# The order of the first units in a fused RWKV attention and cosine router

## Chip, cores and metric

The kernel runs on one core of one Trainium2 chip, in one launch. The metric is device time in microseconds, from the first to the last instruction of a run. The kernel before takes 399.03 us (median of three runs, 398.66 to 399.29).

In the profile PE is TensorE's matmuls and PEld its weight loads, DVE is VectorE, ACT is ScalarE, POOL is GpSimd, and SP is SyncE, which issues the loads. A matmul of float32 appears as two records.

## The reference

An attention with a decaying state, and then a mixture of experts with one expert per token. Cut to what matters:

```python
# r, k, v: (4, 8, 768, 48); w, u: (8, 48)
for t in range(S):
    kt, vt, rt = k[:, :, t], v[:, :, t], r[:, :, t]
    cur = einsum('bhd,bhe->bhde', u * kt, vt)           # the token's own term
    y[:, :, t] = einsum('bhd,bhde->bhe', rt, state + cur)
    state = w * state + einsum('bhd,bhe->bhde', kt, vt)
x = y as rows: (3072, 384)
logits = normalised(x) @ normalised(expert_emb).T / tau   # 8 experts
expert = argmax(logits); gate = softmax(logits)[expert]
out[token] = gate * (relu(x[token] @ w1[expert]) @ w2[expert])
```

## The kernel before

The sequence of 768 is cut into 6 chunks of 128 tokens; with 4 batches that makes 24 units, numbered chunk by chunk. A "step" i works on several units at once: it turns the R and K of unit i+1, sums unit i, scales the K of a coming unit, and ranks the tokens of a group (the four units of one chunk) that was finished some steps earlier. The instructions of each engine run in the order in which the program issues them, and an engine that waits holds everything behind it.

The start loads, computes the powers of the decay, and prepares unit 0:

```python
    wide = k.work.tile([128, 512], F32, name="wide", tag="AT1")
    nc.vector.memset(wide, 1.0)
    def busy(columns):                       # idle products that keep TensorE busy
        ps = k.ps.tile([128, 512], F32, name="wake", tag="y")
        nc.tensor.matmul(ps[:, 0:columns], k.ones, wide[:, 0:columns], start=True, stop=True)
    for _ in range(WAKE):                    # WAKE = 2
        busy(512)
    ...
    load(k, 0, k.Kpad[0])                    # K of unit 0 goes straight to its padded tile
    ...
    own_k(k, 0)
    for p in range(NP):                      # NP = 4: powers of the decay by scans over C = 128
        nc.vector.tensor_tensor_scan(
            t[:, p, :], wc[:, p : p + 1].to_broadcast([128, C]), k.ones, 1.0, ALU.mult, ALU.mult
        )
    ...                                      # mid, kp, rpow, turned K and R of unit 0
    busy(192)
    nc.scalar.copy(k.kpow..., ps...)         # powers by which K is scaled
    nc.vector.tensor_mul(first, first, ps[:, :, :, 0:D])     # K of unit 0, scaled in place
```

The pieces of a step that the change moves or that stand beside them:

```python
def load(k, i, K=None):                      # on SyncE: K, R, (u with unit 0), V
    ...
    if i == 0:
        k.u_bc = ...
        nc.sync.dma_start(out=k.u_bc..., in_=u broadcast to 128 partitions)
    for n in () if i == 0 else (0, 1) if i == 1 else (i,):
        nc.sync.dma_start(out=k.loaded[n][2], in_=of(k.v, n % B))

def scaled(k, i):                            # needs K of unit i and kpow
    k.nc.gpsimd.tensor_mul(k.Kpad[i % 4][:, :, 0:D], k.loaded[i][0], k.kpow)

def own_k(k, i):                             # needs K of unit i and u
    k.nc.gpsimd.tensor_mul(k.KU[i], k.loaded[i][0], k.u_bc)

def own_r(k, i):
    k.nc.gpsimd.tensor_mul(k.KU[i], k.KU[i], k.loaded[i][1][:, :, 0:D])

def own_sum(k, i):
    k.nc.vector.reduce_sum(diag, k.KU.pop(i), axis=AX.X)

def ranks(k, g):                             # PSUM tag "tp": two banks, also of rt, yrows, lgT
    g.rank = k.ps.tile([128, E, B], F32, name="rank", tag="tp")
    mm(g.rank, k.umask, g.oh, start=True, stop=False)
    mm(g.rank, k.ones, g.pre, start=False, stop=True)
```

The step itself, cut (`whole(f, i - n)` runs f for a group whose last unit is i - n; `on(f, i)` runs f for unit i):

```python
    for i in range(-1, units):
        if 0 < i + AHEAD < units:            # AHEAD = 5
            load(k, i + AHEAD)
        whole(places, i - 4)
        ...
        on(turn_r, i + 1)                    # rt: L360, then RT: L362
        if i == 0: own_sum(k, i)
        on(turn_k, i + 1)                    # kt: L369
        ...
        on(scaled, i + 2)                    # L317
        if i < 0:
            own_r(k, 0)
        on(own, i + 2)                       # L328, L332
        ...
        whole(located, i - 4)
        ...
        on(own_sum, i + 1)                   # diag: L337
        on(sums, i)                          # y: L443 (from chunk 1 on), L452
        on(states, i)                        # st: L409
        on(carry, i)                         # state: L422 or L424, then L425 on POOL
        on(scores, i + 1)                    # at: L388
        on(masked, i + 1, 0)                 # AT: L394
        if i == 0: masked(k, i + 1, 1)
        on(rows, i)                          # yrows: L470, then X: L476
        if i != 0: on(masked, i + 1, 1)
        of_group(put, i)                     # X to memory
        of_group(turn_rows, i - 1)           # xp: L556
        whole(logits, i - 2)
        whole(ranks, i - 3)                  # rank: L625, L626
        if i == 0: build_constants(k)        # small memsets on POOL
```

## Time and profile before

| | |
|---|---|
| time | 399.03 us (398.66 to 399.29) |
| span of the profiled run | 396.4 us, 9266 instructions |
| TensorE's granted clock, mean | 0.997 |
| 24 to 36 us: busy PE, DVE, ACT, POOL | 11.73, 9.58, 10.57, 11.59 of 12.00 |
| 113 to 158 us: busy PE, DVE, ACT, POOL | 44.37, 27.46, 19.81, 17.46 of 45.00 |
| 158 to 396 us: busy PE, DVE, ACT, POOL | 232.17, 136.11, 70.88, 53.98 of 238.00 |
| starts of the scores (L388) of units 0 to 4 | 7.50, 11.28, 15.25, 19.55, 23.85 |

The attention takes the first 130 us or so, the experts the rest. A step's length is the distance from one start of the scores to the next. In the table the start is where several engines are full at once, and the experts are TensorE's alone. Shares over the whole span hide this difference: they are read by stretch.

### The profile page before, as it was taken

The page shows a single profiled execution, that of the slowest core. Times are in us where ns is not written, and L with a number is a line of the kernel's source. Part 1 is how long each engine was busy: PE and PEld are TensorE (multiplying, and loading weights), DVE is VectorE, ACT ScalarE, POOL GpSimd, SP SyncE. Part 2 cuts the span into 40 slices and gives each one's busy share as a digit, 9 for nine tenths or more (in the row PEclk, how much of TensorE's full clock was granted, in tenths as well). Part 3 has the DMA queues.
Part 4 walks back from the last instruction along what each step waited for, and adds up shares of the span by engine and source line. Part 5 has one row for each costly group of instructions (what it writes and reads, how often), then busy time and mean ns, then how long its engine had stood idle before and what let it go on. Part 6 is the DMA issues. An engine that isn't in the chain of part 4 may idle for free.

```text
span 396.4 us, 9266 instructions
## 1 busy us (share of the span) xinstructions
PE 386.9 (98%) x3542; PEld 352.5 (89%) x3542; DVE 253.2 (64%) x600; ACT 173.1 (44%) x524; POOL 160.9 (41%) x216
## 2 busy tenths in 40 slices
PE   7999999999999999999999999999999999999993
PEld 4988888889888877899999999999999999799783
DVE  6887878787788670757667668257275456655601
ACT  4887777777677412333333332233323243133120
POOL 7998796858664232500701502220350350200111
PEclk9999999999999999999999999999999999999998
DMA  7899887767606972244705532434164170150111
GB/s 146 163 215 214 189 180 162 157 136 149 142 33 206 288 285 65 87 161 163 255 7 215 196 106 94 133 112 161 55 227 159 43 237 3 40 180 0 41 39 44
DMA packets 93797, 54.35 MB, mean 137 GB/s; under 512 B 76938, under 2 KB 88381, under 8 KB 93747
## 3 DMA queue, kind: packets, MB, share of 16 engines
q1 hardware_dynamic: 90242, 44.26, 41.4%
q0 software_dynamic: 3296, 9.44, 7.3%
q8 instruction: 29, 0.48, 0.5%
q14 instruction: 22, 0.17, 0.1%
q10 hardware_dynamic: 208, 0.00, 0.0%
HBM read 44.45 MB, written 9.63 MB: 136 GB/s over the span
## 4 chain that ended last, share of the span: by engine, by line
PE 86%; SPq 4%; ACT 3%; DMA 2%; DVE 2%; POOL 1%; issue 1%; POOLq 0%; DVEq 0%; ACTq 0%
PE ps L1226 25%; PE ps L1290 18%; PE ps L1330 5%; PE at L388 4%; PE ps L1344 4%; PE y L452 4%; PE early_h L1036 3%; PE early_y L1045 3%; PE ps L1204 3%; PE yrows L470 2%; PE ps L1174 2%; PE y L443 2%; PE rt L360 2%; PE kt L369 2%; PE xp L556 2%; PE st L409 2%
## 5 line engine op out<-in xcount | busy, mean ns | idle before, releaser
L1090 POOL DMA_INDIRECT out_dram<-y,to x25 | 30.1, 1204 | 173.5 <-DVE Sh L1365 109.9
L1226 PE MATMUL ps<-xTe,w 128*128 128x192 f32 (+3 forms) x336 | 62.9, 327 | 0.0
L1226 PEld LDWEIGHTS ps<-xTe,w 128*128 128x128 f32 x336 | 55.9, 190 | 0.5
L346 ACT ACTIVATE xd<-V,diag 128x48 f32<-128x48 f32 x184 | 46.2, 326 | 0.1
L394 DVE TENSOR_TENSOR AT<-at,umask 128x512 f32<-128x512 f32 x48 | 32.7, 685 | 10.5 <-PE at L388 10.3
L1233 ACT ACTIVATE hT<-hT 128x384 f32<-128x384 f32 (+3 forms) x42 | 22.0, 523 | 32.4 <-DVE hT L1256 19.7
L1290 PE MATMUL ps<-Tw,Sh 128*128 128x192 f32 x192 | 32.5, 326 | 0.0
L1290 PEld LDWEIGHTS ps<-Tw,Sh 128*128 128x128 f32 x192 | 31.4, 190 | 0.0
L1081 POOL DMA_INDIRECT G<-xs,take x25 | 27.0, 1080 | 10.5 <-issue 4.6
L1226 PE MATMUL ps<-Tx,Sw 128*128 128x192 f32 (+3 forms) x168 | 29.7, 326 | 0.0
L388 PE MATMUL at<-RT,KT 48*128 48x128 f32 x384 | 27.9, 285 | 0.3 <-DVE RT L362 0.3
L1243 DVE TENSOR_TENSOR u<-ps,p 128x384 f32<-128x384 f32 (+3 forms) x14 | 7.8, 558 | 31.3 <-ACT p L1240 16.6
L1226 PEld LDWEIGHTS ps<-Tx,Sw 128*128 128x128 f32 x168 | 27.6, 190 | 0.1
L452 PE MATMUL y<-AT,V 128*48 128x128 f32 (+1 forms) x384 | 26.0, 278 | 0.0
L388 PEld LDWEIGHTS at<-RT,KT 48*128 48x128 f32 x384 | 23.3, 187 | 2.6 <-issue 0.7
L332 POOL TENSOR_TENSOR KU<-KU,Rpad 128x384 f32<-128x384 f32 x24 | 24.1, 1004 | 1.8
L452 PEld LDWEIGHTS y<-AT,V 128*48 128x48 f32 (+1 forms) x384 | 19.9, 124 | 4.2 <-issue 3.6
L1290 PE MATMUL ps<-w,hT 128*128 128x192 f32 x128 | 23.4, 326 | 0.0
L328 POOL TENSOR_TENSOR KU<-K,u_bc 128x384 f32<-128x384 f32 x23 | 23.2, 1008 | 0.0
L317 POOL TENSOR_TENSOR Kpad<-K,kpow 128x384 f32<-128x384 f32 x23 | 23.1, 1004 | 0.1
L558 ACT COPY xT<-xp 128x384 f32<-128x384 f32 x24 | 11.5, 479 | 25.5 <-PE xp L556 25.5
L1253 ACT ACTIVATE hT<-ps 128x384 f32<-128x384 f32 (+3 forms) x14 | 6.9, 490 | 35.7 <-PE ps L1226 35.7
(240 smaller groups left out, 816.5 us busy)
## 6 DMA issues: line engine op xcount, KB each, us to landing
w<-in_moe_w_dram SPq DMA_DIRECT2D x16, 1536.0 KB, 6.9
Rpad<-in_r_dram SPq DMA_DIRECT2D x24, 192.0 KB, 4.4
V<-in_v_dram SPq DMA_DIRECT2D x24, 192.0 KB, 4.2
xs<-X SPq DMA_DIRECT2D x24, 192.0 KB, 2.7
K<-in_k_dram SPq DMA_DIRECT2D x23, 192.0 KB, 3.7
G<-xs,take POOLq DMA_INDIRECT x27, 3.2
out_dram<-y,to POOLq DMA_INDIRECT x25, 3.5
Kpad<-in_k_dram SPq DMA_DIRECT2D x1, 192.0 KB, 3.2
```

The lines of the kernel that those rows point to most:

```text
L317: k.nc.gpsimd.tensor_mul(k.Kpad[i % len(k.Kpad)][:, :, 0:D], k.loaded[i][0], k.kpow)
L328: k.nc.gpsimd.tensor_mul(k.KU[i], k.loaded[i][0], k.u_bc)
L332: k.nc.gpsimd.tensor_mul(k.KU[i], k.KU[i], k.loaded[i][1][:, :, 0:D])
L346: k.nc.scalar.mul(k.xd[i][:, h, :], V[:, h, :], diag[:, h : h + 1])
L388: nc.tensor.matmul(at[s][:, p, :], KT[rows, p, :], RT[rows, p, :], start=True, stop=True)
L394: k.nc.vector.tensor_mul(a, k.at[i][s], k.umask[:, None, :].to_broadcast([128, NP, C]))
L452: mm(y[s][u * DP : u * DP + n, q, :], V[:, h * D : h * D + n], AT[s][:, p, :], start=(c == 0 and q == 0), stop=True, skip_group_check=True,)
L1081: nc.gpsimd.indirect_dma_start(out=G[0:n, :], out_offset=None, in_=k.xs[:, :], in_offset=IndirectOffsetOnAxis(ap=take[0:n], axis=0), bound ...
L1090: put = k.nc.gpsimd.indirect_dma_start(out=k.out[:, :], out_offset=IndirectOffsetOnAxis(ap=to, axis=0), in_=y, in_offset=None, bounds_chec ...
L1226: nc.tensor.matmul(ps[:, j, :], weights[:, (f + j) * 128 : (f + j + 1) * 128], moving, start=(first and j == 0), stop=True, skip_group_che ...
L1233: nc.scalar.activation(h, h, ACT.Relu)
L1290: nc.tensor.matmul(ps, a[:, f, :], b[:, f, :], start=(first and f == 0), stop=(f == NF // 2 - 1), skip_group_check=True)
```

## The change

The change has five edits.

- A group's rank products, and the two steps that use them (`places`, `located`), move from the end of a step and the head of the next to the middle of that next step, behind the turning of R and K.
- Idle products at the start are made of `ones` (128 columns), nine and later two of them, so that the tile `wide` and its memset go.
- The powers of the decay are scanned over 64 steps, and the other 64 are a product with the 64th power.
- K of unit 0 is loaded into the last padded tile and scaled from there into the first, so that the scaling no longer overwrites what the own term reads. The load of u moves behind V of unit 0.
- The scaling of a K is issued one step earlier (i + 3), ahead of the own term of the unit before it; in the step before the first, the second K is scaled ahead of unit 0's own term.

It is meant to shorten the start and to take a wait out of every fourth step. The core of the diff:

```diff
-WAKE = 2
+WAKE = 9
...
-    def busy(columns):
-        ps = k.ps.tile([128, 512], F32, name="wake", tag="y")
-        nc.tensor.matmul(ps[:, 0:columns], k.ones, wide[:, 0:columns], start=True, stop=True)
-
-    for _ in range(WAKE):
-        busy(512)
+    def busy(count):
+        ps = k.ps.tile([128, 128], F32, name="wake", tag="y")
+        for _ in range(count):
+            nc.tensor.matmul(ps, k.ones, k.ones, start=True, stop=True)
+
+    busy(WAKE)
...
-    load(k, 0, k.Kpad[0])
+    load(k, 0, k.Kpad[3])
...
-    own_k(k, 0)
...
-            t[:, p, :], wc[:, p : p + 1].to_broadcast([128, C]), k.ones, 1.0, ALU.mult, ALU.mult
+            t[:, p, 0:half], wc[:, p : p + 1].to_broadcast([128, half]), k.ones[:, 0:half], 1.0, ALU.mult, ALU.mult
         )
+    nc.vector.tensor_mul(t[:, :, half:C], t[:, :, 0:half], t[:, :, half - 1 : half].to_broadcast([128, NP, half]))
...
-    busy(192)
+    busy(2)
...
-    first = k.Kpad[0].rearrange("q (p s) d -> q p s d", s=2)[:, :, :, 0:D]
-    nc.vector.tensor_mul(first, first, ps[:, :, :, 0:D])
+    raw, first = (t.rearrange("q (p s) d -> q p s d", s=2)[:, :, :, 0:D] for t in (k.Kpad[3], k.Kpad[0]))
+    nc.vector.tensor_mul(first, raw, ps[:, :, :, 0:D])
...
-    if i == 0:
-        k.u_bc = ...                        # load of u, ahead of V
     for n in () if i == 0 else (0, 1) if i == 1 else (i,):
         nc.sync.dma_start(out=k.loaded[n][2], in_=of(k.v, n % B))
+        if n == 0:
+            k.u_bc = ...                    # the same load of u, behind V of unit 0
...
-        whole(places, i - 4)
...
-        on(scaled, i + 2)
         if i < 0:
-            own_r(k, 0)
+            scaled(k, 1)
+            own(k, 0)
+        on(scaled, i + 3)
         on(own, i + 2)
...
-        whole(located, i - 4)
...
         if 0 <= i < units - 2:
             on(own_sum, i + 1)
+        for step in (ranks, places, located):
+            whole(step, i - 4)
...
-        whole(ranks, i - 3)
```

## The prediction

> **What bounds the kernel now.** I read the page first: the busy times, then the chain that ended last.

> ```profile
> PE 386.9 (98%) x3542; PEld 352.5 (89%) x3542; DVE 253.2 (64%) x600; ACT 173.1 (44%) x524; POOL 160.9 (41%) x216
> ...
> PE 86%; SPq 4%; ACT 3%; DMA 2%; DVE 2%; POOL 1%; issue 1%; POOLq 0%; DVEq 0%; ACTq 0%
> ```

> TensorE carries the time. POOL's 41% is an average, though, and the parts of the change lie in two places: the start, and one attention step in four. I therefore asked for busy time by stretch. From 7.5 to 24 us POOL is busy 15.90 of 16.50 us and TensorE 16.34; from 36 to 113 us POOL is busy 56.80 of 77.00 and TensorE 76.91. So in the start both engines are full, and later TensorE alone. The next view is the start in order of time (columns: start, length, engine, line, operation, and in brackets an idle time and what ended it).

> ```profile
> 6.75 1.00 POOL L328 TENSOR_TENSOR KU<-Kpad,u_bc 128x384 f32<-128x384 f32 x1 [1.15 <-DMA u_bc<-in_u_dram]
> ...
> 7.72 1.00 POOL L317 TENSOR_TENSOR Kpad<-K,kpow 128x384 f32<-128x384 f32 x1
> ...
> 8.67 1.01 POOL L332 TENSOR_TENSOR KU<-KU,Rpad 128x384 f32<-128x384 f32 x1
> ...
> 9.64 1.01 POOL L328 TENSOR_TENSOR KU<-K,u_bc 128x384 f32<-128x384 f32 x1
> ...
> 10.72 1.00 POOL L332 TENSOR_TENSOR KU<-KU,Rpad 128x384 f32<-128x384 f32 x1
> ...
> 11.68 0.99 POOL L317 TENSOR_TENSOR Kpad<-K,kpow 128x384 f32<-128x384 f32 x1
> ...
> 11.75 0.55 DVE L337 TENSOR_REDUCE diag<-KU 128x8 f32<-128x384 f32 x1 [0.72 <-POOL KU L332]
> ...
> 12.49 1.28 DVE L394 TENSOR_TENSOR AT<-at,umask 128x512 f32<-128x512 f32 x2
> ...
> 13.79 1.09 PE L452 MATMUL y<-AT,V 128*64 128x128 f32 x16
> ...
> 16.02 1.00 POOL L317 TENSOR_TENSOR Kpad<-K,kpow 128x384 f32<-128x384 f32 x1
> ...
> 19.10 0.55 DVE L337 TENSOR_REDUCE diag<-KU 128x8 f32<-128x384 f32 x1 [0.29 <-POOL KU L332]
> ...
> 20.53 1.01 POOL L317 TENSOR_TENSOR Kpad<-K,kpow 128x384 f32<-128x384 f32 x1
> ```

> POOL's row of products has no hole from 6.75 us on, and VectorE waits for it at 11.75 and 19.10: the sum "diag" of unit 1, then of unit 3. VectorE works in order, so the masks AT behind "diag" wait too, and the matmuls L452 behind them. In the start, what delays POOL's own terms (KU) delays TensorE.

> The third view is a step in which a group is ranked.

> ```profile
> 42.06 0.49 PE L556 MATMUL xp<-ident,X 128*128 128x128 f32 x3
> ...
> 42.33 0.56 DVE L476 TENSOR_TENSOR X<-yrows,xd 128x384 f32<-128x384 f32 x1
> 42.39 0.31 PE L625 MATMUL rank<-seq,umask 128*128 128x32 f32 x2
> ...
> 42.53 0.39 PE L626 MATMUL rank<-run,ones 128*128 128x32 f32 x2
> ...
> 42.94 0.66 PE L360 MATMUL rt<-ident,Rpad 128*128 128x128 f32 x4
> ```

> The turned R (rt) starts 0.41 us after the second rank product. X, which reads yrows, ends at 42.89. Yrows, rank and rt take the two banks of one tag in turn, so rt stands in the bank that X is still reading.

> [...]here a scan of 128 starts every 0.355 us (1.42/4), 2.8 ns per element, against 0.69 us or 1.35 ns for the product of 512[...]. [...]here K's bars are 0.4 to 1.0 us and K lands 4.2 us after issue (median of the first 40 us), so I count from landings. [...]

> **The change, part by part.** The order of instructions on each engine, with the changed kernel set against this one, shows four things.

> *Ranks a turn later.* In four steps the two rank products move behind rt and kt, so rt follows xp at once and takes the other bank. Now: rank start to rt start 42.94 - 42.39 = 0.55, and 0.06 more before kt. Behind kt, four weight loads and short products remain, estimated at 0.4 from the two passes of the count product (108.62 to 108.84 us, 0.22). Gain 0.61 - 0.4 = 0.2 a step, 0.8 in all, on TensorE in its full stretch, so on the path.

> *Idle products and powers.* The 512-wide memset (0.48) goes, so the idle products start about 0.5 earlier. Instead of 2 x 512 columns they do 9 x 128: 1152 for 1024, and end where they did. Four scans of 64 at some 0.2, plus a product of 256 elements at 0.35, replace 1.42: some 0.2 gained, so the first scores start at about 7.3 and not 7.5.

> *Loads.* u goes behind V of unit 0. K, R and V of units 0 and 1 land, by the trace's landing records, at K 4.62, R 5.66, u 6.61, K 7.59, R 8.69, V 9.57, V 10.30; then K of unit 2 at 11.56, of unit 3 at 15.95, of unit 4 at 19.14. With u three places later, K and R of unit 1 and V of unit 0 land 1 us sooner, and u at 9.57.

> *POOL's order.* The diff speaks of the second K. But `scaled, i + 2` became `scaled, i + 3`, so every own term now stands behind the scaling of a K one unit younger. POOL's queue becomes K1, own 0, K2, own 1, K3, own 2, state, K4, own 3. With a scaling 0.97 and an own term 2.0 (from the starts above):
> - K1 7.4 to 8.4; own 0 waits for u: 9.6 to 11.6; K2 (landed 11.56) to 12.6; own 1 to 14.6, before 11.7.
> - Diag of unit 1 then starts at 14.65 instead of 11.75. Diag 0.55, state 0.35, mask 0.65: L452 of unit 1 at 16.2 instead of 13.79, 2.4 later. TensorE idles some 2.4 us.
> - K3 not before 15.95: to 16.95; own 2 to 19.0, before 14.7. State 0.5 and the constants 0.85: 20.3. K4 to 21.3, own 3 to 23.3, before 19.07 (the diag at 19.10). That is 4.2 later; less the 0.3 that VectorE gains on its own work there, TensorE is some 4.0 behind.
> - After that K5 (landed at about 22.3) and later are there in time. POOL needs some 3.9 a step and TensorE 4.3 and more, so the lag grows no further; nor is it made up, since TensorE is full.

> K3's landing decides the size: 15 of its 16 parts were there by 14.4 and one came 1.5 later. If the late part comes in time, K3 starts at 14.6 and the lag is 3.0. I take 3.6, in which the earlier scores of unit 0 are swallowed, since own 1 sets the masks of unit 1. Sum: 399.0 + 3.6 - 0.8 = 401.8 us.

> **The rivals.** (a) It works as the words say: unit 1's K and R come sooner, the first product no longer waits for POOL's read of the raw K (0.34 before L112), 0.2 comes from the powers. Then -0.3 and -0.8: 397.9. For it: rt of unit 1 waits 0.33 for its input at 8.79. Against it: the own term of unit 1, which gates the masks, gets later by a scaling and a landing. (b) The lag comes, but is made up in the steps from 24 to 36 us, where ScalarE is busy 10.57 of 12.00 and TensorE idles 0.27: at most 0.3 to recover, so 401.5. (c) The idle gaps make the clock fall to half for some microseconds: 2 to 4 us more, 404 to 406. The gaps speak against it, and TensorE's granted clock was 1.00 in every stretch. (d) The shorter look-ahead for K (used two steps after its load's turn and not three) bites all along. Against it: the scaling at 74.08 us uses a K issued at 59.01, so a step less leaves some 6 us over.

> **Range and chances.** K3 early gives 401.2, K3 late and a little less from the ranks 402.6; one more hold in the start gives 403. The lower side must allow that POOL's wait is partly hidden by something I read wrongly, such as u landing sooner: 399.9. So 399.9 to 403.2. Two per cent is 8.0 us; neither (a) nor (c) reaches it. Faster by over 2%: 0.01; within: 0.97; slower: 0.02.

> **What would show it.** In the changed profile: POOL idle before its first own term for u (about 1.2) and before the scaling of K3 (about 1.3); VectorE's diag of unit 1 at about 14.7 with a wait of some 3 for POOL, the diag of unit 3 at about 23.4; L452 of unit 1 at 16.2; scores of unit 4 at about 27.7 instead of 23.85; rt right behind xp in every step and a rank step of 5.3 instead of 5.5. I am wrong if diag of unit 1 starts before 13, if the four later scores run at the old times, or if POOL finds its K there at once.

## The result and the profile after

The changed kernel takes 402.35 us (median of six runs, 401.61 to 402.79) against 398.56 for the kernel before beside it (six runs, 398.01 to 399.29). The ratio is 1.0091, 95% interval 1.0077 to 1.0106: 3.8 us more, which is less than 2%. The profiled spans are 400.4 and 396.4 us. The change takes one line out, so line numbers of the changed kernel are one lower (L388 is now L387).

The page first: busy times, the row of the granted TensorE clock in 40 slices of 10 us, and the chain that ended last.

```profile
PE 389.4 (97%) x3558; PEld 357.4 (89%) x3558; DVE 251.8 (63%) x600; ACT 172.6 (43%) x524; POOL 161.6 (40%) x216
...
PEclk9899999999999999999999999999999999999999
...
PE 89%; ACT 3%; DVE 2%; POOL 2%; issue 1%; DMA 1%; SPq 1%; POOLq 0%; DVEq 0%; ACTq 0%
```

TensorE is busy 2.5 us longer than before for the same work. About 0.7 of it is idle products (4.82 us in all instead of 4.07; the 16 more records are theirs, as eleven of 128 columns stand for three wider ones), the rest slower products. The second slice of the clock row shows an 8 where the rest shows 9: the clock fell, which the kernel before never had between 5 and 394 us. In the chain POOL went from 1% to 2%, and PE from 86% to 89%.

The start in order of time (start, length, engine, line, operation, and in brackets an idle time of the engine and what ended it):

```profile
9.81 1.01 POOL L327 TENSOR_TENSOR KU<-Kpad,u_bc 128x384 f32<-128x384 f32 x1 [0.90 <-DMA u_bc<-in_u_dram]
...
12.82 1.00 POOL L327 TENSOR_TENSOR KU<-K,u_bc 128x384 f32<-128x384 f32 x1
...
13.89 0.99 POOL L331 TENSOR_TENSOR KU<-KU,Rpad 128x384 f32<-128x384 f32 x1
...
14.92 0.55 DVE L336 TENSOR_REDUCE diag<-KU 128x8 f32<-128x384 f32 x1 [2.43 <-POOL KU L331]
...
15.32 1.00 POOL L316 TENSOR_TENSOR Kpad<-K,kpow 128x384 f32<-128x384 f32 x1 [0.43 <-DMA K<-in_k_dram]
...
15.65 1.28 DVE L393 TENSOR_TENSOR AT<-at,umask 128x512 f32<-128x512 f32 x2
...
15.88 0.63 PE L368 MATMUL kt<-ident,Kpad 128*128 128x128 f32 x4 [2.38 <-DVE state L421]
...
16.44 1.70 PE L451 MATMUL y<-AT,V 128*64 128x128 f32 x16
...
17.92 1.04 PE L408 MATMUL st<-V,Kpad 128*48 128x48 f32 x16
...
18.40 0.55 DVE L336 TENSOR_REDUCE diag<-KU 128x8 f32<-128x384 f32 x1 [0.41 <-POOL KU L331]
...
18.89 1.76 PE L387 MATMUL at<-RT,KT 48*128 48x128 f32 x16
...
22.96 0.54 DVE L336 TENSOR_REDUCE diag<-KU 128x8 f32<-128x384 f32 x1
...
23.79 1.16 PE L387 MATMUL at<-RT,KT 48*128 48x128 f32 x16
...
28.84 1.16 PE L387 MATMUL at<-RT,KT 48*128 48x128 f32 x16
```

POOL stands idle for u (0.90) until 9.81. Its own term for unit 1 (the KU lines at 12.82 and 13.89) ends at 14.88, and VectorE's sum "diag" starts at 14.92 after 2.43 of waiting; before, it started at 11.75. The copy of the state (L421) stands behind diag on VectorE, and kt takes the PSUM tag that this copy empties ("st"), so TensorE waits 2.38 us ahead of kt, and L451 of unit 1 starts at 16.44 instead of 13.79. Then its products take 1.70, 1.04 and 1.76 us; in the kernel before y and the scores took 1.09 and 1.16, as the scores do again here at 23.79. That is the clock: half of it was granted from 16.76 to 20.17. Busy times for this stretch of 3.41 us and for those of the same length before and behind it (columns: stretch, its length, busy time and count of PE, PEld, DVE, ACT, POOL, then the granted clock, the DMA share and GB/s):

```profile
13.35:16.76 3.41, 1.03 (x12) 0.74 (x12) 1.84 (x4) 1.29 (x6) 2.90 (x4) 1.00 0.65 120
16.76:20.17 3.41, 3.41 (x43) 3.22 (x40) 2.50 (x10) 2.71 (x11) 3.27 (x17) 0.50 1.09 207
20.17:23.58 3.41, 3.41 (x54) 3.12 (x52) 2.82 (x5) 2.03 (x7) 3.33 (x5) 1.00 0.97 207
```

In the 3.41 us from 13.35 to 16.76 TensorE worked 1.03 us. The next 3.41 us ran at half clock, with TensorE busy all of it.

The starts of the scores add the story up. Each difference is after less before, from the lines "at" in the two traces.

| unit | 0 | 1 | 2 | 3 | 4 | 7 | 8 | 12 | 16 | 20 to 23 |
|---|---|---|---|---|---|---|---|---|---|---|
| after less before, us | +0.24 | +0.09 | +3.64 | +4.24 | +4.99 | +4.99 | +4.75 | +4.51 | +4.26 | +4.10 |

- Own term of unit 1 late: L451 of unit 1 16.44 - 13.79 = 2.65.
- Half clock: 0.99 more up to the scores of unit 2 (3.64 - 2.65), and 0.60 inside these scores (4.24 - 3.64); 1.59 together. This is how much longer the products took; what a full clock gives back is measured below, and is less.
- Small operations on VectorE: 0.75 more from unit 3 to unit 4, shown next.
- Ranks: -0.24 three times and -0.16 once, -0.9 in all.

2.65 + 1.59 + 0.75 - 0.9 = 4.1, and the spans differ by 4.0.

The third item is in the step of unit 3:

```profile
24.12 1.00 POOL L316 TENSOR_TENSOR Kpad<-K,kpow 128x384 f32<-128x384 f32 x1
24.19 0.96 DVE L201 CAST own<-bits 128x3 f32<-128x3 int32 x1
...
25.08 0.99 POOL L327 TENSOR_TENSOR KU<-K,u_bc 128x384 f32<-128x384 f32 x1
...
25.18 0.92 DVE L202 TENSOR_TENSOR own<-own 128x1 f32<-128x1 f32 x1
...
26.02 0.68 DVE L393 TENSOR_TENSOR AT<-at,umask 128x512 f32<-128x512 f32 x1
...
26.16 1.00 POOL L331 TENSOR_TENSOR KU<-KU,Rpad 128x384 f32<-128x384 f32 x1
```

The "own" lines belong to small tables that the kernel builds in steps 1 to 5 (128 rows of 3 elements or 1). In the kernel before each took 0.16 us. Here the first ends at 25.15 and the second at 26.10, just when POOL's products end (25.12 and 26.07), and the mask AT, on which the next TensorE products wait, stands behind them.

Last, the step in which a group is ranked:

```profile
47.05 0.49 PE L555 MATMUL xp<-ident,X 128*128 128x128 f32 x3
47.38 0.60 PE L359 MATMUL rt<-ident,Rpad 128*128 128x128 f32 x4
47.82 0.60 PE L368 MATMUL kt<-ident,Kpad 128*128 128x128 f32 x4
48.26 0.31 PE L624 MATMUL rank<-seq,umask 128*128 128x32 f32 x2
48.40 0.39 PE L625 MATMUL rank<-run,ones 128*128 128x32 f32 x2
48.72 0.65 PE L442 MATMUL y<-RT,state 48*64 48x128 f32 x16
```

Rt now follows xp by 0.33 us, kt follows, and the two rank products lie behind. The step from one start of the scores to the next (45.52 to 50.76) is 5.24 instead of 5.48.

### The profile page after: what moved, and what is told of

The parts are those of the page before. It is cut to its first block, busy times and chain, and to the rows that moved or that the text cites. A ratio compares the mean times of both kernels' runs of the same rounds, so it can differ in the third digit from the quotient of the medians.

```text
span 400.4 us, 9319 instructions
## 1 busy us (share of the span) xinstructions
PE 389.4 (97%) x3558; PEld 357.4 (89%) x3558; DVE 251.8 (63%) x600; ACT 172.6 (43%) x524; POOL 161.6 (40%) x216
## 4 chain that ended last, share of the span: by engine, by line
PE 89%; ACT 3%; DVE 2%; POOL 2%; issue 1%; DMA 1%; SPq 1%; POOLq 0%; DVEq 0%; ACTq 0%
PE ps L1225 25%; PE ps L1289 18%; PE ps L1329 5%; PE at L387 5%; PE y L451 5%; PE ps L1343 4%; PE early_h L1035 3%; PE yrows L469 3%; PE early_y L1044 3%; PE ps L1203 3%; PE ps L1173 2%; PE y L442 2%; PE rt L359 2%; PE kt L368 2%; PE st L408 2%; PE xp L555 2%
## 5 line engine op out<-in xcount | busy, mean ns | idle before, releaser
L1080 POOL DMA_INDIRECT G<-xs,take x25 | 28.1, 1125 | 10.5 <-issue 4.3
L387 PE MATMUL at<-RT,KT 48*128 48x128 f32 x384 | 28.5, 289 | 0.0
L451 PE MATMUL y<-AT,V 128*48 128x128 f32 (+1 forms) x384 | 26.8, 282 | 0.5 <-DVE AT L393 0.4
L387 PEld LDWEIGHTS at<-RT,KT 48*128 48x128 f32 x384 | 23.9, 191 | 2.1 <-issue 0.7
L451 PEld LDWEIGHTS y<-AT,V 128*48 128x48 f32 (+1 forms) x384 | 20.2, 125 | 5.1 <-issue 3.6
L557 ACT COPY xT<-xp 128x384 f32<-128x384 f32 x24 | 11.5, 479 | 27.7 <-PE xp L555 27.7
L1289 PE MATMUL ps<-w,hT 128*128 128x192 f32 x128 | 23.4, 326 | 0.0
```

What stands on the lines that cost most here:

```text
L387: nc.tensor.matmul(at[s][:, p, :], KT[rows, p, :], RT[rows, p, :], start=True, stop=True)
L451: mm(y[s][u * DP : u * DP + n, q, :], V[:, h * D : h * D + n], AT[s][:, p, :], start=(c == 0 and q == 0), stop=True, skip_group_check=True,)
L1080: nc.gpsimd.indirect_dma_start(out=G[0:n, :], out_offset=None, in_=k.xs[:, :], in_offset=IndirectOffsetOnAxis(ap=take[0:n], axis=0), bound ...
L1289: nc.tensor.matmul(ps, a[:, f, :], b[:, f, :], start=(first and f == 0), stop=(f == NF // 2 - 1), skip_group_check=True)
```

## The experiments

The theories:

- **A**: POOL's queue. An own term behind the scaling of a K that hasn't landed, or behind a u that comes late, opens the hole on TensorE.
- **B**: the late u alone does it.
- **C**: the half clock after the hole is a cost of its own.
- **D**: the new head (idle products, powers in two halves) brings something in itself.
- **E**, formed after the first runs: the small tables beside POOL's dense row cost the rest, and built later they would cost nothing.

Every kernel does the whole computation; where one adds idle products, that is said. Times are medians beside the kernel before on the same chip, whose own median goes from 399.19 to 399.86; the expectations of the first four runs start from 398.56, so they are compared as differences. The differences of score starts are against the profile of the kernel before shown above, so some 0.2 to 0.9 of them at the first units can be later landings of the loads (the first run below shows how much).

### Ranks alone

The kernel before, with one part of the change:

```diff
-        whole(places, i - 4)
...
-        whole(located, i - 4)
+        for step in (ranks, places, located):      # behind the turning of R and K
+            whole(step, i - 4)
...
-        whole(ranks, i - 3)
```

> The kernel before with the moved rank products alone. Both theories: the four rank steps get 0.24 shorter (the last one 0.16), the start is as before: 398.56 - 0.9 = 397.7 us. If the ranks only swap one wait for another, 398.5.

Measured: 399.11 against 399.86 us, ratio 0.998 (0.9973 to 0.9987), -0.75. In its trace the first own term waits for u until 7.95 us instead of 6.75, and the second K lands at 8.55 instead of 7.58. The scores are +0.83 at unit 2, which these landings account for as far as is known, and the ranked steps take it from +0.92 at unit 7 to +0.02. So the moved ranks are worth 0.8 to 0.9.

### The scaling back in its place, u late

The changed kernel, with the scaling of a K at its old distance:

```diff
-        on(scaled, i + 3)
+        if i >= 0:
+            on(scaled, i + 2)
```

> The changed kernel with the scaling back at i + 2 (order on GpSimd: K1, own 0, own 1, K2, own 2); u still late. Theory A (the queue of GpSimd sets the start: own 1 ends where u's landing at 9.8 and 4 us of own terms put it, about 13.9 and not 14.9): diag of unit 1 at 13.9, about 1 us less than the changed kernel, 401.3; if the hole on TensorE is then too short for the clock to fall, down to 400.0. Theory B (u's late landing sets everything and the order is harmless): 402.3, as changed.

Measured: 402.00 against 399.86, ratio 1.0046 (1.003 to 1.0063). POOL waits 1.69 us for u, starts its first own term at 10.29, and the diag of unit 1 starts at 14.44. The clock falls from 15.63 to 19.04. Scores of unit 2 are +3.77. VectorE waits 1.48 us for it, and TensorE's kt of unit 2 waits 1.79 us for the scaled K, which here stands behind that own term. The late u opens the hole without the new scaling. As differences, A had put +2.7 us and B +3.7; measured is +2.1, although diag came later than A's 13.9 and the clock fell.

### u back in its place, the scaling early

The changed kernel, with the load of u moved ahead of V of unit 0 again.

```diff
     if i == 0:
+        k.u_bc = ...                        # load of u
...
-        if n == 0:
-            k.u_bc = ...
```

> The changed kernel with the load of u back in third place; the scaling still at i + 3. Theory A: own 1 stands behind the scaling of K2, which lands at 11.5; diag of unit 1 at about 14.6 instead of 14.9; 402.0. Theory B (u's landing is what GpSimd lacks): diag of unit 1 back near 12 and the time near 398.

Measured: 402.82 against 399.86, ratio 1.0077 (1.0064 to 1.009). The trace of this kernel, POOL and the diag of unit 1:

```profile
9.53 1.01 POOL L328 TENSOR_TENSOR KU<-Kpad,u_bc 128x384 f32<-128x384 f32 x1
...
12.00 0.99 POOL L317 TENSOR_TENSOR Kpad<-K,kpow 128x384 f32<-128x384 f32 x1 [0.39 <-DMA K<-in_k_dram]
...
15.06 0.55 DVE L337 TENSOR_REDUCE diag<-KU 128x8 f32<-128x384 f32 x1 [2.86 <-POOL KU L332]
```

The first own term no longer waits for u. But the scaling of K of unit 2 waits for its landing (0.39), the own term of unit 1 stands behind it, and diag starts at 15.06. Scores of unit 2 are +4.37. B, the late u alone, falls: either half of the new order is enough, and the two do not add.

### Ten idle products in the hole

The changed kernel, with ten idle products of 128 columns behind rt of unit 2. They are extra work, and only fill the wait.

```diff
+        if i == 1:
+            k.busy(10)
```

> The changed kernel with ten more idle products (2.3 us) on TensorE between rt and kt of unit 2, in the hole of 2.5 us that it has there. Theory A: the granted clock stays at 1.00, but own 3 on GpSimd still ends at about 22.6, so that only some 0.3 to 0.5 comes back: 401.9. Theory C (the half clock from 16.6 to 20.0 us is what costs, the queue only opens the hole): the 1.6 us by which the products of unit 1 and the scores of unit 2 were longer come back: 400.7.

Measured: 402.36 against 399.86, ratio 1.0069 (1.0054 to 1.0084). TensorE in its trace, and the diag of unit 3:

```profile
13.37 2.40 PE L66 MATMUL wake<-ones 128*128 128x128 f32 x20
16.33 0.63 PE L369 MATMUL kt<-ident,Kpad 128*128 128x128 f32 x4 [0.56 <-DVE state L422]
16.89 1.28 PE L452 MATMUL y<-AT,V 128*64 128x128 f32 x16
...
18.53 1.16 PE L388 MATMUL at<-RT,KT 48*128 48x128 f32 x16
...
22.90 0.55 DVE L337 TENSOR_REDUCE diag<-KU 128x8 f32<-128x384 f32 x1 [0.81 <-POOL KU L332]
...
27.12 1.16 PE L388 MATMUL at<-RT,KT 48*128 48x128 f32 x16
```

The idle products ("wake") fill 2.40 us, the clock stays at 1.00, and y and the scores behind the hole take 1.28 and 1.16 instead of 1.70 and 1.76. Scores of units 2 to 4 are +3.28, +3.28, +3.27: the hole without the clock. Here diag of unit 3 waits 0.81 for POOL, and still the scores of unit 4 are no later than those of unit 2: TensorE has no gap from 17 to 31 us. At unit 7 it is +4.05, because a small operation of the tables (tie, 0.16 us in the changed kernel's trace) took 2.81 beside two of POOL's products. Against the changed kernel's ratios (1.0091 and, below, 1.0103) the gain is 0.9 to 1.4 us of 400. The intervals of these ratios overlap (1.0077 to 1.0106 and 1.0081 to 1.0125 against 1.0054 to 1.0084), so the times alone would not settle it. The traces do: the lag at unit 3 is 3.28 instead of 4.24, and at the last unit 3.15 instead of 4.10. C holds: the clock is a cost of its own. About 0.95 of its 1.59 comes back, between what A alone leaves to it and what C gave; the hole itself was wider in this trace (L452 of unit 1 at 16.89 instead of 16.44).

### The changed kernel on another chip

> The changed kernel once more, as the measure for the runs beside it on the same chip: 3.8 us above the kernel before (ratio 1.009), scores of unit 4 some 4 to 5 us late.

Measured: 403.28 against 399.39, ratio 1.0103 (1.0081 to 1.0125). Diag of unit 1 at 15.94, half clock from 17.18 to 20.59, scores of unit 2 +5.13. The same picture, with u landing later.

### The kernel before with only the new POOL order

The scaling at i + 3 and the second K ahead, u early, K of unit 0 in the last padded tile; no moved ranks, old head.

```diff
-    load(k, 0, k.Kpad[0])
+    load(k, 0, k.Kpad[3])
...
-        on(scaled, i + 2)
         if i < 0:
+            scaled(k, 1)
             own_r(k, 0)
+        on(scaled, i + 3)
```

> The kernel before with the longer look-ahead of the scaling alone (K1 as before between the halves of own 0, then K2 ahead of own 1, and so on); u in its old place, no moved ranks. Theory A (an own term behind a scaling whose K has not landed is enough to open the hole): own 1 ends at 14.6 instead of 11.7, 3 to 4.5 us above before. Theory B (only u's late landing does it): within 0.5 of before.

Measured: 403.33 against 399.39, ratio 1.0093 (1.008 to 1.0106): +3.9, within what A put. POOL and the diag of unit 1:

```profile
7.66 1.00 POOL L328 TENSOR_TENSOR KU<-Kpad,u_bc 128x384 f32<-128x384 f32 x1 [2.10 <-DMA u_bc<-in_u_dram]
...
12.12 1.00 POOL L317 TENSOR_TENSOR Kpad<-K,kpow 128x384 f32<-128x384 f32 x1 [1.53 <-DMA K<-in_k_dram]
...
15.18 0.55 DVE L337 TENSOR_REDUCE diag<-KU 128x8 f32<-128x384 f32 x1 [3.62 <-POOL KU L332]
```

K of unit 2 is waited for 1.53 us at the head of the queue, and VectorE waits 3.62. From unit 3 on the scores are +4.49, and still +4.50 at the last unit: the loss stays in the first three units, and nothing is made up or added after. The shorter look-ahead does not cost later (rival d of the prediction).

### Both parts undone

The changed kernel with u early and the scaling at i + 2 (both diffs above); the second K is still scaled ahead of unit 0's own term.

> The changed kernel with both undone: u in third place, scaling at i + 2; but K1 is still scaled ahead of the whole own term of unit 0. Theory A: GpSimd waits for the powers until about 7.6 to 8.5 and then has K1, own 0, own 1 in a row, own 1 ends some 1.2 us later than before; with 0.9 from the ranks 0.3 above before. Theory B: 0.9 below before.

Measured: 399.54 against 399.39, ratio 1.0003 (0.9994 to 1.0011). Diag of unit 1 is back at 13.66, scores of unit 2 at +1.54, the clock full. On the same chip the kernel of the next section stands at +0.79 at unit 2, so some 0.75 of the loss is left. The one scaling (1.00 us) that still stands ahead of unit 0's own term is its likely place; no run moves that scaling alone. The hole is undone: A is confirmed, and B's 0.9 below before did not come.

### Ranks and the new head, old POOL order

The kernel before's order of POOL and of the loads, with the moved ranks, the idle products of 128, the scans of 64 and the raw K in the last padded tile. The order of POOL against the kernel before (the same instructions in the same order, written otherwise):

```diff
-        on(scaled, i + 2)
         if i < 0:
+            scaled(k, 1)
             own_r(k, 0)
+        if i >= 0:
+            on(scaled, i + 2)
```

> Before's queue on GpSimd and before's order of loads, with the moved ranks, the idle products of 128 columns, the scans of 64 and the scaling out of the raw tile. Theory A: the start is bound by the loads and GpSimd, the shorter powers give nothing: 0.9 below before, as the ranks alone. Rival D (the head counts once the queue is right): 1.2 to 1.4 below before.

Measured: 398.56 against 399.39, ratio 0.9979 (0.997 to 0.9988), -0.83. The ranks alone gave 0.998. So the head brings nothing that these runs can tell from zero, and D falls. This kernel and that of the ranks alone beat both kernels, by 0.2%.

### The tables later

In four kernels the small tables' pieces of steps 2 to 5 are built in steps 12 to 15, when POOL is busy less:

```diff
-        if 0 < i < B + 2:
+        if i == 1 or 12 <= i < 16:
             next(tables)
```

In the changed kernel:

> The changed kernel with VectorE's small operations on tables (own, mask, turned, tie) moved from the steps 2 to 5 to the steps 12 to 15, where GpSimd has holes. Theory E (beside a dense row of GpSimd's products these operations of 0.16 us take 0.9 and more, and they stand ahead of the masks): the step from unit 3 to unit 4 gets 0.8 shorter, 3.0 above before instead of 3.8. Theory F (they are only late with everything else): 3.8 above before.

In the kernel with ten idle products:

> The changed kernel with both: ten idle products in the hole on TensorE, and the tables later. What is then left is the queue of GpSimd alone. Theory A with 3.0 to 3.3 late from the queue and 0.9 gained by the ranks: 2.1 to 2.4 above before. If clock and tables are only symptoms: 3.8 above.

In the kernel of ranks and head:

> The version with before's queue, the moved ranks and the new head, and the tables later. The mask of 1.65 us beside GpSimd's products stood ahead of the masks of unit 4: theory E 1.2 below before; theory F 0.85 below, as without it.

In that one, with memsets of POOL's constants (caps, sums, fresh) at step 5 too:

> The same, and 0.6 us of small memsets on GpSimd (caps, sums, fresh) moved from step 0 to step 5. VectorE waits 0.3 to 0.8 for GpSimd's own terms of units 3 and 4: theory A (GpSimd's queue sets the start) 0.3 to 0.6 more, 1.6 below before; if TensorE is full anyway, 1.2 below before.

Measured, all against 399.19: 406.84, ratio 1.0165 (1.0144 to 1.0186); 402.75, 1.0096 (1.0075 to 1.0117); 399.68, 1.0009 (1.0001 to 1.0018); 399.71, 1.0019 (1.0011 to 1.0026). No gain in any of the four times: E fails as a remedy. Where it went is plain in the third of them, in step 13 (POOL's and VectorE's lines and the TensorE product behind them):

```profile
73.81 2.35 DVE L203 TENSOR_TENSOR own<-own 128x1 f32<-128x1 f32 x1
...
75.15 1.00 POOL L329 TENSOR_TENSOR KU<-K,u_bc 128x384 f32<-128x384 f32 x1
...
76.08 0.68 DVE L395 TENSOR_TENSOR AT<-at,umask 128x512 f32<-128x512 f32 x1
76.22 1.00 POOL L333 TENSOR_TENSOR KU<-KU,Rpad 128x384 f32<-128x384 f32 x1
...
76.82 0.64 PE L453 MATMUL y<-AT,V 128*48 128x128 f32 x8 [0.68 <-DVE AT L395]
```

"own" has one element per row. It starts at 73.81, while POOL multiplies the state (from 73.72) and then its products follow one another from 74.19 on, and ends at 76.16, when the second of them ends (76.15) and before the next begins at 76.22. AT waits behind it, and TensorE for AT (0.68, and 0.42 once more). In all four kernels this one operation took 2.35 to 2.36 us, and the step to unit 14 is 1.35 to 1.37 longer. POOL is busy less here, but not in this microsecond. Before that step, moving the tables away brought what E had put where they had been held: in the changed kernel the step from unit 3 to unit 4 takes 4.30 instead of 5.05, and in the kernel with idle products the lag at unit 7 is +3.36 instead of +4.05. In the kernel of ranks and head it brought nothing: from unit 2 to unit 4 that kernel loses 0.11 with them and 0.13 without them.

The fourth kernel shows the same elsewhere. With the constants gone, POOL's next scaling starts at once:

```profile
15.75 1.00 POOL L322 TENSOR_TENSOR Kpad<-K,kpow 128x384 f32<-128x384 f32 x1
...
16.13 1.59 DVE L223 COPY cum<-ebase 1x8 f32<-1x8 f32 x1
...
16.70 1.00 POOL L333 TENSOR_TENSOR KU<-K,u_bc 128x384 f32<-128x384 f32 x1
...
17.83 0.67 DVE L399 TENSOR_TENSOR AT<-at,umask 128x512 f32<-128x512 f32 x1
```

The copy "cum" (8 elements in one row, 0.16 us in the changed kernel's trace) takes 1.59 and ends with POOL's product, at 17.72 and 17.70; AT is late, and the scores of unit 3 are at +1.10, where the third kernel has +0.55. The fifteen runs of this kernel form two groups, eight from 399.39 to 399.71 and seven from 400.35 to 400.74. The profiled run took 400.35 and belongs to the second, so the hold on "cum" is shown for a run of that group alone.

The first of the four, at 406.84, has a larger cause. Its windows (columns as above):

```profile
12.12:15.53 3.41, 1.39 (x12) 0.82 (x9) 0.59 (x2) 1.91 (x8) 3.27 (x4) 1.00 0.94 181
15.53:18.94 3.41, 2.48 (x18) 2.18 (x20) 3.35 (x7) 1.35 (x5) 3.30 (x4) 0.50 0.87 173
18.94:22.36 3.42, 3.42 (x39) 3.11 (x36) 0.99 (x8) 1.67 (x7) 3.28 (x17) 0.50 1.14 195
22.36:25.77 3.41, 3.41 (x19) 3.08 (x21) 2.82 (x5) 1.09 (x4) 1.67 (x4) 0.50 1.18 238
25.77:29.18 3.41, 3.41 (x58) 3.23 (x56) 1.40 (x4) 2.85 (x12) 3.25 (x5) 1.00 1.21 240
```

Own term, diag (15.50) and kt came later on this chip, TensorE worked 1.39 of 3.41 us in one window and 2.48 in the next, and the clock stayed at half for three windows, 10.24 us, instead of one. The scores are +4.95 at unit 2 instead of the changed kernel's +3.64, and +7.53 at unit 3 instead of +4.24. So most of its extra cost is the later hole with its longer half clock, and 1.36 the step of "own". Its five runs go with the clock: 404.58 us at a mean of 0.992, 405.15 at 0.988, 406.84 to 407.06 at 0.983.

## Why the prediction was right, and where not

The predicted 401.8 was 0.5 low, but it started from 399.0 for the kernel before, where the runs beside the changed kernel gave 398.56: the growth was put at 2.8 us and came to 3.8. The sign and the main cause, POOL's queue, were right. That the number came as near as it did is in part luck: one term of the sum did not come, and two that were not in it took its place. Its steps:

1. **POOL's queue.** "K1, own 0, K2, own 1, K3, own 2" is the order in the trace. Diag of unit 1 was put at 14.65 and L452 of unit 1 at 16.2; measured 14.92 and 16.44. TensorE's idle time was put at 2.4; measured 2.38. The experiments that undo one half, the other and both confirm this cause. Its two halves do not add, which the prediction did not say.
2. **K of unit 3.** The prediction left open whether K3 comes at 14.4 or at 15.95, lag 3.0 or 4.0, and took 3.6. K3 was scaled at 15.32 after 0.43 of waiting, between the two; the own term of unit 3 ended at 22.66 and not at 23.3, and diag 3 (22.96) no longer waited for POOL, because the half clock had made TensorE late enough by itself. With the clock held up by idle products, diag 3 did wait for POOL (0.81), and the lag stayed at 3.27: it had been there since unit 2, and K3 added nothing. So the term of 1.2 for K3 failed. The prediction counted a wait of VectorE as a wait of TensorE. In the kernel before, too, the wait of 0.29 at 19.10 left no gap on TensorE, which has none over 0.12 us from 14 to 30 us.
3. **Rival (c), the clock.** Here the prediction failed: "The gaps speak against it". It took its gap of about 2.4 us for too short. That, and the "2 to 4 us more" that it set on the rival, were its author's estimates; no trace had shown how long a gap leaves the clock full. In the changed kernel's trace the full clock is recorded from 6.52 us on, and half from 16.76 to 20.17: after 10.24 us, which is three times 3.413, and for 3.413. In the last of the three, from 13.35 to 16.76, TensorE worked 1.03 us, and the half clock came behind it. The products took 1.59 longer for it, of which about 0.95 came back with a full clock; neither is the "2 to 4 us more" of that rival. The trace of the kernel before had one case to read: TensorE ends there at 390.17 us, and its clock falls to half at 394.09.
4. **"The lag grows no further".** It grew by 0.75 once, from unit 3 to 4, by VectorE's small operations beside POOL; with the tables built later that step was 0.75 shorter (4.30 instead of 5.05). POOL was full there before, too, and one of them (mask) was held 1.66 us in the kernel before. The delay of the start shifted which of the small operations met which of POOL's products.
5. **Ranks.** Put at 0.2 a step and 0.8 in all; measured 0.24, 0.24, 0.24 and 0.16, 0.9 in all, and 0.75 as a time alone. A rank step was put at 5.3 for 5.5; measured 5.24 for 5.48.
6. **Head.** The first scores were put at 7.3; they came at 7.74, and at 7.4 to 8.0 in the other runs with this head. The full clock is recorded from 6.52 on in the changed kernel's profile and from 4.97 on in that of the kernel before; the first kt and rt, at 5.19 and 6.04, took 1.06 and 0.84 us, where they took 0.60 and 0.63 in the kernel before. As the prediction said, this is swallowed, and the kernel of ranks and head shows that it is worth nothing either way.

So the lag, put at 2.4 + 1.2 = 3.6, was 5.0: the hole itself 2.65 for 2.4; nothing for K3 instead of 1.2; 1.59 from the clock and 0.75 from the small operations, which were not in the sum. The time grew by 3.8 and not by the 4.1 of the starts; runs of one kernel differ by 1.2 to 1.3 here, which covers that. The scores of unit 4, put at 27.7, came at 28.84.

Open: why the clock stayed at half for three windows of 3.41 us in one kernel, when the second of them was already full of work (3.42 of 3.42 us) and the third was no fuller. It is also open how well the mean clock of a single run tells its time. Of the kernel with u late, the one run at 0.998 took 400.35 and those at 0.992 to 0.994 took 401.84 to 402.60; of the kernel with u early, the one run at 0.999 took 403.47 and those at 0.992 to 0.994 took 402.72 to 403.08. In the second set of runs of the changed kernel it goes with the time (402.11 at 0.993, 405.47 at 0.985), and in the kernel with only the new POOL order it does not (403.49 at 0.999, 402.95 to 403.60 at 0.994). What a run loses when its clock does not fall is in none of these traces.

## What to carry to other kernels

When an engine works its queue in order, moving a piece that needs a late load ahead of a piece that another engine waits for is a bet on that load: set every piece's landing beside its place in the queue before counting what the piece costs. Where the trace shows the clock fall behind a hole on TensorE, count the hole twice, once as the wait and once as what the clock costs (2.38 us of waiting and 1.59 us of longer products here); a few idle products in the hole bought part of the second back here (about 1 us of 400). A mean of POOL's busy time does not tell whether a small VectorE operation placed there will be held ("own", 0.16 us elsewhere, took 2.35 in step 13, where POOL was busy less): look at the very microseconds. And a wait on one engine is a cost only where the trace shows the bounding engine idle behind it: with the idle products diag of unit 3 waited 0.81 us, and the scores of unit 4 lagged by 3.27, no more than those of unit 2 (3.28).

## What the runs showed of the hardware

**VectorE beside POOL.** The small operations own, cum, mask and tie, which take 0.16 to 0.22 us alone, took up to 2.81 us when they fell on POOL's products (0.92, 0.96, 1.59, 1.66, 2.35 and 2.81), ending each time within 0.04 us of the end of one. It was not always the next to end: "own" at 73.81 and "tie" at 38.48 (to 41.29) ended with the second of two products that followed one another, while the cast to "own" in the changed kernel (24.19 to 25.15) ended with the first (25.12), with the next begun at 25.08. Not every operation is held: the sum "diag" (a reduction of 384 elements) never took more than 0.56, and a reciprocal (0.14 us at 27.68, within POOL's product from 27.58 to 28.58) and an integer operation "bits" (0.13 us at 19.64, within the product from 19.61 to 20.61), both in the changed kernel, took no longer than elsewhere. The held ones were a product of two tensors (own), a cast (own), a copy (cum) and operations on a tensor (mask, tie); what sets them apart from those not held is not shown here.
